# The last 64 of 320 features contracted in row pairs, in two layers of an mLSTM and mixture-of-experts kernel

## The chip, the cores and the metric

The kernel runs on one core of one Trainium2 chip. The metric is the time of one execution on the device in microseconds (us), as the median of several runs.

## The reference, cut to what matters

An mLSTM attention (batch 4, 8 heads, 768 steps, head size 40) gives 3072 tokens of 320 features. A dense layer with a leaky ReLU follows, and then a layer of 8 experts of which each token takes one:

```python
def _moe_ref(x, w_in, w_out, alpha):           # 3072 x 320, 320 x 2048, 2048 x 320
    h = x @ w_in
    g = np.maximum(h, 0.0) + alpha * np.minimum(h, 0.0)
    return g @ w_out
def _moe2_ref(x, w_gate, w_output_gate, w1, w2):   # 8 experts, 320 x 1024 and 1024 x 320
    ...
        h = np.maximum(x[mask] @ w1[e], 0.0)
        ye = h @ w2[e]
        out[mask] = gate_w[mask, None] * eom[mask, e, None] * ye
```

## The kernel before, in words

**Precision.** A product is made of three: each operand is split into a rounded high part and the rest (low part), and high times high, low times high and high times low are added in PSUM, each as one pass of TensorE over float32 operands marked float32r. Plain float32 products, as in the attention, take two passes each.

**The 320 features.** They fill two and a half blocks of 128 rows. In the two first products (`ffn1`, L928, and `slot_1`, L402) block 2 of the tokens holds the last 64 features twice: their high part in rows 0 to 63, their low part in rows 64 to 127. The weights hold the last 64 rows twice as well (`dup`, L1362). So one product over 128 rows does high and low at once, and each first product takes 8 passes (`PASSES`, L926) instead of 9:

```python
PASSES = ((0, 0, 0), (1, 1, 0), (2, 2, 0), (3, 0, 0), (4, 1, 0), (0, 0, 1), (1, 1, 1), (2, 2, 1))
```

**First phase.** The attention runs in 24 units of 128 tokens; three units make a block of 384 tokens, 8 blocks in all. For each block 16 chunks of 128 hidden features pass through the dense layer, 128 chunks in all, by these steps: `F` (`ffn1`, 8 products of 384 columns into one of two PSUM tiles `ph`), `f` (`ffn_act`, L941: ScalarE's ReLU of the negative, then VectorE's sum), `g` (`ffn_split`, L951: the high part on ScalarE, the low part on VectorE or GpSimd) and `S` (`ffn2`, L957: 9 products of 336 columns). Up to chunk 24 (`KEEP`) the activated values stand in SBUF, after that in the tile `ph`, which is then held until `g` has read it. Attention's own steps stand between these: `as` (`att_s`, L756) multiplies queries and keys over 40 rows, alternately in rows 0 to 39 and rows 64 to 103, so that neighbouring products lie in different halves of the array's rows and go to different PSUM tiles; `ah` (`att_h`, L778) takes 120 rows and `ab` (`att_b`, L853) tiles of 32 columns. The weights of the dense layer come as 64-bit words that VectorE puts together (`words`, L647) and are split into both parts, and the experts' weights are loaded, split and stored again as high and low parts in a DRAM scratch (`el`, `es`, `et`).

The order of all these steps on every engine is one written list (`ORDER`, L96), and `OTHER` (L50) names the steps that go to the less usual engine.

**Second phase.** The tokens are gathered by expert into slots of 128. A slot j runs `slot_1` (two halves of 512 hidden columns, 8 products of 512 columns each, tokens stationary, weights moving out of a ring of three experts in SBUF), then TensorE does `slot_2` of slot j-1 (24 products of 320 columns) and `slot_t` of slot j (8 transposes, L414), and `slot_x` (L381) transposes the tokens of slot j+2. The offset of the expert in the ring is a register. `next_load` (L344) fetches the next expert into the ring by two conditional loads per slot, on SyncE's queue. 28 slots run.

Of the kernel before, what the change touches and what calls it, by code (L numbers as in the profile page):

```python
# [17 lines left out]
P = 128  # L18
# [6 lines left out]
E = 8  # L25
# [3 lines left out]
EC = 3 * F2 + 8 * DM  # L29
RC = 2 * EC  # L30
R1 = 6 * F2
# [5 lines left out]
HELD = 22  # L37
PIECES = [(c, 768, c, 3 * F2) for c in range(0, 3 * F2, 768)]
PIECES += [(3 * F2 + c, 640, R1 + c, 8 * DM) for c in range(0, 8 * DM, 640)]
NPIECE = len(PIECES)  # L40
PC = 768
# [3 lines left out]
KEEP = 24  # L45
# [6 lines left out]
        4, 5, 7, 8, 10, 11, 13, 15, 19,  # L52
    ),
    "prep_kt": (
        1, 2, 3, 7, 8, 10, 13, 14, 15, 16,
    ),
    "att_y": (
        4, 5, 8, 11, 13, 16, 17, 18, 19, 20, 21, 22, 23,
    ),
    "expert_split": (  # L60
        0, 1, 8, 9, 11, 12, 13, 14, 15, 18, 19, 20, 25, 26, 27, 30, 31, 32, 33, 34, 35, 36, 37, 38, 39,
        40, 41, 42, 43, 44, 45, 46, 47, 48, 49, 50, 51, 52, 53, 54, 55, 56, 57, 58, 59, 60, 61, 62, 63,
    ),
    "att_n": (
        3, 4, 5, 8,
    ),
    "att_r": (
        5, 7,
    ),
    "att_u": (  # L70
        0, 2, 3, 4, 6,
# [4 lines left out]
        0, 4, 6, 7, 11,  # L76
    ),
    "split_wo": (
        0, 3, 6, 8, 9, 12, 15,
# [15 lines left out]

ORDER = """  # L96
load_gates load_cst lo load_sel ga do gb lo lo do do do load_wg lq gw lv lo gm gates_st do do lv so gc gv ge gs gt
so gates_d do gw gc do do do so gw do do gc gt li lo gv pt gw so do di di load_g load_g gs di li ad gv gc lg gv
load_g li ae si ah au di gs as di load_g di gs ae si ae ae do ah am pt do di an an ab aa di di ay so ay lq as si gw
ay ay log av am lo do sg lg do load_g do ad au av ab aa gc ay ay li lo ac do ay ay ay ae ax ah an so do do gw gc lq  # L100
as di di di load_g ae gw lv am ay load_g ab aa ay li pt si ae gc ac ay ay ay lv ax gv lo lo log ay load_g load_g gs
do do so load_g gv do li gs lo so gv do ac gw set_al1 do ax F gs di do F el ae gw ae di di f si lq lq lg gc di di f
ad gc di gv gv g so gs S F do lo ae gs lv do as au do av si F f am ah pt ad es g do do g do so lo do do do F an et
f f gw gc ab aa load_cst2 li li au av lo so S gw S lg ay ay di ay F gw so load_g gc ay di g gv di di di di g gv li
gs gs gc si si do do pt sg ay di S do f g S log di di si as F F li li am so di gw ah di di gv li li gc gs f gv S di
di an ad si lq f di di ab lo lg lg pt lv F au F av li load_g g S g load_g sg load_g ac si f di di aa f g gs si F F
lv lg ah S S ad ay ax ay di di di di ah ae ay ay as si do do load_g g S ae an do gw f di ay ae di gc g F am si f li
ac ax lq lq gv gs ab aa F g f ay lo pt S ae di S ae li ay ay load_g ay as lq lo di di ay g S ac ad av am so ab aa
au f si F di lg g S lq el do av lg load_g load_g di di ax do do au ah f do do do si load_g el gw F an F an gw el f
ay F ay ay so es gc gv gc gv ay lv as so gs g g f ay S gs ae es S am f ae et et bo F F lv ac el as lq g g S ae F pt  # L110
log f f F el lq g ae am ad ab ab F g ax f f load_g load_g au es et av ah F bp aa ay el ay es et S ay an pt ay aa S
S g S ad ay g f g es lv lv f ac ax au F F S ae S f et f g ay es ay load_g el av as g g pt am F el ah ay ay sg an ab
et es es S F S F et el S f lq g el ay ac lg et ad F F f g es et f g f f el S g S S S au av aa load_g el ay ay es es
ay pt ah an ax lg g ay ay pt et lg ae es F f S et g F f log ad au av g ae et as am ae S bo F f g F f load_g ae ab
aa ay el lv el S g ay es el F f as am g load_g load_g es et es et F f load_g ac ax lv ah an el el ae ae lg lg S g S
S F f g ad au av pt ah an ay es F f g ab aa F f ay ay ad au av et ae et S g el load_g el F f es ay et F f ay ay ac
ax S g es ae S g ah an F f S S et es ay ay et g lv el el bp as am F f F f el g es et pt S S ab aa ac ax g ad au av
F f F f g S g ay lq sg es es S ay lv pt F f ay el lq g F f as am S g F f et es ah an ad au av S log S g bo F f sg
et g load_g load_g ay ay el el F f lg S ae ab aa ay ay ay et S F f S g lq lq S g ae ac ax lg el S as am lv load_g
load_g load_g es et es et ay ay F f pt F f g g ab aa ae ay ac ax F f S g es ay ay ay ay S F f F f ae as am lq S g g  # L120
load_g ah an ad au av ac ax ae el F f lv pt el ae g et ab aa ay ay S es es F f et et g load_g ay F f S g as am ay
ay lv S load_g S F f g F f ah an ab aa ay S el el es ad au av lg ay ae g ay el es F f ac ax g load_g et et ah an ah
an lv es et ae bp ay ay S S S ae as am F f g F f load_g bo g ab aa ae load_g ae F f g S lq el S ac ax F f g load_g
pt S pt F f lg load_g ae as am el es lq F f S g S el g es et F f et g ay ay el F f ae ab aa g ay ay ay ay F f
load_g lv F f S lq S ad au av g g es et es et el ad au av pt ae ac ax S F f g S el el as am F f F f log g S S g es
et lg bp es et F f F f g S g S load_g el S es et F f g F f log el el ae ay ay g S S bo es F f lg F f ah an g S es
as am sg ay ay et et g F f g lq ab aa ay S F f g el el S es load_g load_g sg F f F f S g ay ad au av g es ae ac ax
et S lv et ay ay ay pt F f es F f ah an ab aa ay ay lg el ae g S g es ay lv ad au av pt S F f F f el g ac ax ah an
et es et S load_g ay ay ae g el el F f es S g lg S ad au av F f et es F f lq et et g el el ac ax bp S g S S F f g F
f S es es g F f g et S S bo as am el es F f F f g et lv pt el el et as am ab aa ay es et ay ay load_g S S g lg el  # L130
load_g first_set ah an lq ab aa el ay ay ay F f g F f S g ad au av ae es F f F f lv es g S g ac ax S S ae ay ay ay
ay as am et et es et ac ax F f g F f S el el el bp g F f ah an ab aa g es es ay ay ay ay ay F f F f S S S g g et es
et el S et el F f g F f el S es es g F f et et ac ax g S S es et F f g ld el el F f g S F f g S bo ld es F f F f S
g g route_a S F f F f S g el g S bh bh bh et ld ld ld ad au av bh ld ld bh bh bh F f ld S ld es S ld ld g es F f g
bh bh S bh bh F f g F f S et bh ld g ld S bp F f F f ld bh g bh bh bh bh S S bh route_first bh bh bh g F f
route_first2 first_rows S g F f g ld S F f F f S ld ld g S ld ld ld pt ld ld g first_x first_x S bo bp et first_1
route_b first_1 route_c first_t first_s first_tl route_c2 first_t first_tl first_s first_2 first_2 route_d first_st
first_2 first_2
# [79 lines left out]
def mlstm_moe_kernel(  # L218
# [102 lines left out]
    def ring_mm(j, q, o_, lhsT, off, col, n, start, stop):  # L321
        if off is None:
            col += j * RC
        r = ring[:, col : col + n] if off is None else ring[:, ds(off + col, n)]
        mm = T.matmul(o_, lhsT, r, start=start, stop=stop)  # L325
        if j >= NB:
            return
        if j < 2:
            for ld in loads.values():
                tc.declare_no_dep(mm.ins, ld.ins, reason="the second expert has another slot, so its place is not loaded yet")  # L330
            return
        if j < 4:
            for ld in third:
                tc.declare_no_dep(mm.ins, ld.ins, reason="the first two experts have four slots or more")
        for jj in range(j - 3, j + 3):
            for qq in range(2):
                if (jj, qq) in loads and (jj, qq) != (j - 3, q):
                    tc.declare_no_dep(mm.ins, loads[jj, qq].ins, reason="that load is for other products")
        if (j - 3, q) in loads:
            tc.add_manual_dep(mm.ins, loads[j - 3, q].ins.name, SYNC, reason="weights of this slot")  # L340
# [40 lines left out]
    def slot_x(j):  # L381
        x = slot_rows(j)
        pt = (ps_acc if j > 1 else ps_att)(f"xt_{j}")
        for k in range(3):
            T.transpose(pt[:, k * P : (k + 1) * P], x[:, k * P : (k + 1) * P], ident)
        xh = work("xh", j, [P, 384], F32R, 3)
        xl = work("xl", j, [P, 256], F32R, 3)
        A.activation(xh, pt[:, :384], AF.Copy)
        V.tensor_tensor(xl, pt[:, :256], xh[:, :256].bitcast(F32), ALU.subtract)
        V.tensor_tensor(xh[64:128, 256:], pt[64:128, 256:384], xh[64:128, 256:].bitcast(F32), ALU.subtract)  # L390
        sl_x[j] = (x, xh, xl)
# [1040 lines left out]
```

## Time and profile before

| | |
|---|---|
| median of 3 runs | 745.13 us (744.65 to 745.71) |
| profiled execution | 743.45 us, its span 741.7 us |
| granted TensorE clock, mean | 0.991 of full speed |
| busy: TensorE products, weight loads | 97%, 91% of the span |
| busy: VectorE, ScalarE, GpSimd | 62%, 50%, 25% |

The span is the time from the first to the last instruction; the execution's time has 1.75 us around it. PE is TensorE's products, PEld its weight loads, which overlap products. The recorded duration of a product includes its passage through the array, so the rate of a row of products is read from the distance of their starts, not from that duration.

### The profile page before, as it was taken

The page shows a single profiled execution, that of the slowest core. Times are in us where ns is not written, and L with a number is a line of the kernel's source. Part 1 is how long each engine was busy: PE and PEld are TensorE (multiplying, and loading weights), DVE is VectorE, ACT ScalarE, POOL GpSimd, SP SyncE. Part 2 cuts the span into 40 slices and gives each one's busy share as a digit, 9 for nine tenths or more (in the row PEclk, how much of TensorE's full clock was granted, in tenths as well). Part 3 has the DMA queues.
Part 4 walks back from the last instruction along what each step waited for, and adds up shares of the span by engine and source line. Part 5 has one row for each costly group of instructions (what it writes and reads, how often), then busy time and mean ns, then how long its engine had stood idle before and what let it go on. Part 6 is the DMA issues. An engine that isn't in the chain of part 4 may idle for free. (4 is left out here: it accounts for less than half of the span.)

```text
span 741.7 us, 18086 instructions
## 1 busy us (share of the span) xinstructions
PE 716.8 (97%) x6347; PEld 673.2 (91%) x6347; DVE 456.9 (62%) x1115; ACT 373.0 (50%) x870; POOL 183.9 (25%) x239
## 2 busy tenths in 40 slices
PE   5889999999999999999999999999999999999996
PEld 4679989999999999899999999998999999999996
DVE  6889987768676667677787877766333222332222
ACT  4767878747646546646644554433333322333232
POOL 1543455422303232100100100022222222232223
PEclk9979999999999999999999999999999999999999
DMA  8968779898897947769887788886966726911000
GB/s 249 289 208 283 222 211 293 290 287 315 260 339 240 311 156 267 247 237 308 264 283 283 247 283 319 288 299 234 421 241 265 289 103 267 420 55 39 32 14 23
DMA packets 81527, 179.57 MB, mean 242 GB/s; under 512 B 8620, under 2 KB 39209, under 8 KB 80156
## 3 DMA queue, kind: packets, MB, share of 16 engines
q1 hardware_dynamic: 77980, 169.66, 67.2%
q0 software_dynamic: 3456, 8.71, 3.5%
q8 instruction: 56, 0.92, 0.5%
q14 instruction: 35, 0.29, 0.1%
HBM read 246.29 MB, written 55.59 MB: 407 GB/s over the span
## 5 line engine op out<-in xcount | busy, mean ns | idle before, releaser
L932 PE MATMUL ph<-ring 128*128 128x384 f32 x1024 | 199.2, 343 | 3.2 <-DVE ring L954 2.7
L932 PEld LDWEIGHTS ph<-ring 128*128 128x128 f32 x1024 | 177.5, 189 | 8.4 <-DVE ring L954 5.1
L966 PE MATMUL acc<-ring 128*128 128x336 f32 x384 | 123.2, 326 | 0.2 <-ACT ring L953 0.2
L967 PE MATMUL acc<-ring 128*128 128x336 f32 x384 | 119.5, 317 | 0.0
L945 ACT ACTIVATE v<-ph 128x384 f32<-128x384 f32 x128 | 62.4, 489 | 89.4 <-PE ph L932 88.3
L445 DVE TENSOR_SCALAR yo<-po,xg 128x320 f32<-128x320 f32 x26 | 14.3, 551 | 137.4 <-PE po L325 137.4
L325 PE MATMUL po<-ring,hh 128*128 (+1 forms) x432 | 95.6, 308 | 0.0
L947 DVE SCALAR_TENSOR_TENSOR ph<-v,al,ph 128x384 f32<-128x384 f32 x104 | 63.8, 617 | 44.3 <-ACT v L945 44.0
L325 PE MATMUL p<-ring,xh 128*128 (+1 forms) x324 | 89.8, 398 | 0.0
L969 PE MATMUL acc<-ring 128*128 128x336 f32 x384 | 80.2, 317 | 0.3 <-DVE ring L954 0.3
L325 PEld LDWEIGHTS po<-ring,hh 128*128 128x128 f32 x432 | 73.2, 187 | 2.3 <-ACT hh L425 0.2
L966 PEld LDWEIGHTS acc<-ring 128*128 128x128 f32 x384 | 72.2, 188 | 2.1 <-ACT ring L953 0.5
L954 DVE TENSOR_TENSOR ring<-ph,ring 128x384 fp32r<-128x384 f32 x104 | 57.2, 553 | 26.0 <-ACT ring L953 24.6
L953 ACT ACTIVATE ring<-ph 128x384 fp32r<-128x384 f32 x104 | 50.5, 488 | 45.1 <-DVE ph L947 40.9
L425 ACT ACTIVATE hh<-p 128x512 fp32r<-128x512 f32 x54 | 29.4, 595 | 86.4 <-PE p L423 86.4
L967 PEld LDWEIGHTS acc<-ring 128*128 128x128 f32 x384 | 72.2, 188 | 0.0
L325 PEld LDWEIGHTS p<-ring,xh 128*128 128x128 f32 x324 | 58.8, 188 | 11.3
L446 POOL DMA_INDIRECT out_dram<-yo,tok x28 | 28.1, 1003 | 160.9 <-DVE yo L445 129.6
L412 ACT ACTIVATE hr<-p 128x512 f32<-128x512 f32 x56 | 33.4, 597 | 67.7 <-PE p L325 67.7
L325 PE MATMUL po<-ring,hl 128*128 (+1 forms) x216 | 66.6, 308 | 0.2 <-DVE hl L427 0.2
L969 PEld LDWEIGHTS acc<-ring 128*128 128x128 f32 x384 | 63.5, 189 | 0.6 <-DVE ring L954 0.6
L753 ACT ACTIVATE D<-D,EKT 128x128 f32<-128x128 f32 x192 | 60.7, 394 | 5.1 <-DMA D<-gd 5.0
(211 smaller groups left out, 1102.5 us busy)
## 6 DMA issues: line engine op xcount, KB each, us to landing
ring<-scr SPq DMA_DIRECT2D x26, 3072.0 KB
ring<-scr SPq DMA_DIRECT2D x26, 2560.0 KB
ring<-scr SPq DMA_DIRECT2D x33, 512.0 KB
D<-gd SPq DMA_DIRECT2D x48, 256.0 KB
er<-in_ew_dram SPq DMA_DIRECT2D x32, 384.0 KB
scr<-ring SPq DMA_DIRECT2D x32, 384.0 KB
scr<-er SPq DMA_DIRECT2D x32, 384.0 KB
er<-in_ew_dram SPq DMA_DIRECT2D x32, 320.0 KB
```

The source lines that it names most:

```text
L325: mm = T.matmul(o_, lhsT, r, start=start, stop=stop)
L412: A.activation(hr_half(j, hf), ph, AF.Relu)
L425: A.activation(hh[:, hs], pts[j, hf], AF.Copy)
L753: A.activation(d[:, j], d[:, j], AF.Exp, bias=EKT[:, c, i + j : i + j + 1])
L932: T.matmul(ph[:, :384], wi_[i][lo][:, wc], xTs[n % 2][:, xc], start=(a == 0), stop=(a == len(PASSES) - 1),)
L945: A.activation(v, ph[:, :384], AF.Relu, scale=-1.0)
L947: V.scalar_tensor_tensor(g, v, al1[:, i : i + 1], ph[:, :384], ALU.mult, ALU.add)
L953: A.activation(gh, v, AF.Copy)
L954: engine(V, G, "ffn_split", k).tensor_tensor(gl, v, gh.bitcast(F32), ALU.subtract)
L966: T.matmul(ac, gh[:, sl], hi, start=(i == 0), stop=False)
L967: T.matmul(ac, gh[:, sl], lo, start=False, stop=False)
L969: T.matmul(accs[n][t][:, :NO], gl[:, t * P : (t + 1) * P], hi, start=False, stop=(i == NFC - 1))
```

## The change

The last 64 features are no longer doubled. Weights of two halves of the output now share a block of 128 rows: rows 0 to 63 hold the last 64 features' weights for one, rows 64 to 127 for the other. The tokens' block 2 holds the last 64 features twice in the high part and twice in the low part. Three products per output (`ENDS`) run over 64 rows, those of the two outputs alternately, so that neighbours lie in different halves of the array's rows and in different PSUM tiles; six products per output (`PAIRS`) run over 128 rows. In the dense layer the two outputs are an even chunk and the odd one after it, in an expert slot the two halves of 512 columns. In slots from 2 on ScalarE first copies the ends' weights (128 x 1024) from the ring to a tile at a fixed place (`slot_e`).

With it come: smaller weights (2048 + 512 in place of 3072 columns of each part of an expert's first matrix; odd chunks of the dense layer 256 in place of 384 columns); all activated values in SBUF (`KEEP` 128); one subtraction in place of two in `att_x` and `slot_x`; more buffers for `v` and `raw`; a new `ORDER`, and new lists in `OTHER` (60 of the 128 low parts of `ffn_split` on GpSimd, 9 before). In the new order the TensorE step directly ahead of an odd chunk's `F` is `as` 9 times, `ab` 2 times and an even `F` 33 times of 64, and no even `F` follows directly on an odd one.

```diff
-EC = 3 * F2 + 8 * DM
+W1 = 2 * F2
+WE = F2 // 2
+EC = W1 + WE + 8 * DM
-HELD = 22
-PIECES = [(c, 768, c, 3 * F2) for c in range(0, 3 * F2, 768)]
+HELD = 20
+PIECES = [(0, 704, 0, W1), (704, 704, 704, W1), (1408, 640, 1408, W1), (W1, WE, 2 * W1, WE)]
-KEEP = 24
+KEEP = 128
...
+PAIRS = ((0, 0, 0), (0, 1, 0), (1, 0, 0), (1, 1, 0), (0, 0, 1), (0, 1, 1))
+ENDS = ((0, 0), (1, 0), (0, 1))
...
+    def slot_e(j):
+        at = nc.values_load(roff[0:1, j - 1 : j], engines=[ET.Activation], min_val=0, max_val=2 * RC, **KW)
+        ends[j] = we[j % 2]
+        cp_ = A.activation(ends[j], ring_at(j, at, 2 * W1, 2 * WE).bitcast(F32), AF.Copy)
+        ring_dep(j, 0, cp_.ins)
...
-        chunks = (xh[:, 0:P], xh[:, P : 2 * P], xh[:, 2 * P :], xl[:, 0:P], xl[:, P:])
+        chunks = [t[:, c * P : (c + 1) * P] for t in (xh, xl) for c in range(3)]
         for hf in halves:
             ph = ps_att(f"p1_{j}_{hf}")
-            for a, (xc, wc, lo) in enumerate(PASSES):
-                ring_mm(j, 0, ph, chunks[xc], offs[j], lo * 3 * F2 + wc * F2 + hf * 512, 512, a == 0, a == len(PASSES) - 1)
-            A.activation(hr_half(j, hf), ph, AF.Relu)
+            p1s[j, hf] = ph
+            if hf:
+                for a, (l_, lo) in enumerate(ENDS):
+                    for h_ in range(2):
+                        rows = slice(64 * h_, 64 * h_ + 64)
+                        es = slice(lo * WE, (lo + 1) * WE)
+                        r = ring_at(j, None, 2 * W1 + lo * WE, WE, rows) if j < 2 else ends[j][rows, es]
+                        mm = T.matmul(
+                            p1s[j, h_], chunks[3 * l_ + 2][rows], r, start=(h_ == 1 and a == 0), stop=(h_ == 0 and a == 2)
+                        )
+                        if j < 2:
+                            ring_dep(j, 0, mm.ins)
+                A.activation(hr_half(j, 0), p1s.pop((j, 0)), AF.Relu)
+            for a, (l_, wc, lo) in enumerate(PAIRS):
+                ring_mm(
+                    j, 0, ph, chunks[3 * l_ + wc], offs[j], lo * W1 + wc * F2 + hf * 512, 512,
+                    hf == 0 and a == 0, hf == 1 and a == len(PAIRS) - 1,
+                )
+            if hf:
+                A.activation(hr_half(j, 1), p1s.pop((j, 1)), AF.Relu)
+                ends.pop(j, None)
+                if 2 <= j and j + 1 < NB:
+                    slot_e(j + 1)
...
         def load_wi(i):
-            load_words(f"wi{i}", wi[i], 3 * P)
+            n = (3 - i % 2) * P
+            load_words(f"wi{i}", wi[i // 2, :, i % 2 * 3 * P : i % 2 * 3 * P + n], n)
...
-            V.tensor_tensor(xT[:, 3:5, cols], pv[:, 0:2], xT[:, 0:2, cols].bitcast(F32), ALU.subtract)
-            V.tensor_tensor(xT[64:128, 2, cols], pv[64:128, 2], xT[64:128, 2, cols].bitcast(F32), ALU.subtract)
+            V.tensor_tensor(xT[:, 3:6, cols], pv, xT[:, 0:3, cols].bitcast(F32), ALU.subtract)
...
         def ffn1(k):
             n, i = divmod(k, NFC)
-            ph = ps_h(f"ph_{k}")
-            for a, (xc, wc, lo) in enumerate(PASSES):
+            x = xTs[n % 2]
+            gt[k] = ps_h(f"ph_{k}")
+            odd = i % 2
+            if odd:
+                for a, (l_, lo) in enumerate(ENDS):
+                    for o in range(2):
+                        rows = slice(64 * o, 64 * o + 64)
+                        T.matmul(
+                            gt[k - 1 + o][:, :384],
+                            wi_[i - 1][lo][rows, 2],
+                            x[rows, 3 * l_ + 2],
+                            start=(o == 1 and a == 0),
+                            stop=(o == 0 and a == 2),
+                        )
+            for a, (l_, wc, lo) in enumerate(PAIRS):
                 T.matmul(
-                    ph[:, :384],
+                    gt[k][:, :384],
                     wi_[i][lo][:, wc],
-                    xTs[n % 2][:, xc],
-                    start=(a == 0),
-                    stop=(a == len(PASSES) - 1),
+                    x[:, 3 * l_ + wc],
+                    start=(odd == 0 and a == 0),
+                    stop=(odd == 1 and a == len(PAIRS) - 1),
                 )
```

## Rows read from the trace of the kernel before

**Rows 1.** The page: busy time, share of the span, instructions; granted clock in 40 slices

```profile
PE 716.8 (97%) x6347; PEld 673.2 (91%) x6347; DVE 456.9 (62%) x1115; ACT 373.0 (50%) x870; POOL 183.9 (25%) x239
...
PEclk9979999999999999999999999999999999999999
```

**Rows 2.** Busy time by stage: stage, its length, busy of each engine, clock, DMA

```profile
0.00:20.00 20.00, 9.57 (x129) 7.66 (x129) 13.02 (x40) 9.40 (x28) 4.10 (x10) 1.00 0.85 253
20.00:40.00 20.00, 17.58 (x219) 14.61 (x223) 18.50 (x42) 13.56 (x34) 10.68 (x14) 0.87 0.92 270
40.00:60.00 20.00, 17.57 (x272) 15.20 (x265) 18.06 (x47) 14.20 (x45) 8.62 (x12) 0.87 0.80 238
60.00:490.00 430.00, 426.42 (x4231) 410.27 (x4230) 324.65 (x785) 256.52 (x616) 96.95 (x134) 1.00 0.82 272
510.00:735.00 225.00, 224.83 (x1374) 206.78 (x1373) 67.98 (x144) 71.22 (x134) 56.95 (x57) 1.00 0.49 192
```

**Rows 3.** What TensorE's products waited for: total us, times, longest

```profile
PE pe_g L576 <- DVE gin L572: 6.9, 1, 6.9
PE ph L932 <- DVE ring L954: 2.7, 8, 0.7
```

**Rows 4.** Timeline of PE around one att_s: start, us, engine, line, count

```profile
302.64 1.57 PE L932 MATMUL ph<-ring 128*128 128x384 f32 x8
304.14 1.16 PE L763 MATMUL ps<-q 40*128 40x128 f32 x16
305.23 1.68 PE L932 MATMUL ph<-ring 128*128 128x384 f32 x8
306.75 0.32 PE L966 MATMUL acc<-ring 128*128 128x336 f32 x1
```

**Rows 5.** Timeline of PEld around the same att_s, two answers

```profile
302.49 1.40 PEld L932 LDWEIGHTS ph<-ring 128*128 128x128 f32 x8
304.14 0.97 PEld L763 LDWEIGHTS ps<-q 40*128 40x128 f32 x16 [0.25 <-issue]
...
304.25 0.86 PEld L763 LDWEIGHTS ps<-q 40*128 40x128 f32 x14
```

**Rows 6.** Timeline of PE around one att_h, 120 rows

```profile
168.03 0.83 PE L785 MATMUL pb<-state,qg 120*128 120x123 f32 x6
168.62 1.65 PE L932 MATMUL ph<-ring 128*128 128x384 f32 x8
170.11 0.31 PE L966 MATMUL acc<-ring 128*128 128x336 f32 x1
```

**Rows 7.** Timeline of PEld in expert slots: transposes, then products of 512 columns

```profile
604.58 0.94 PEld L423 LDWEIGHTS p<-cst,hr 128*128 128x128 f32 x8
...
606.85 1.34 PEld L325 LDWEIGHTS p<-ring,xh 128*128 128x128 f32 x6
```

**Rows 8.** Groups by line and shape: busy us, mean ns, idle before and its releaser

```profile
L945 ACT ACTIVATE v<-ph 128x384 f32<-128x384 f32 x128 | 62.4, 489 | 89.4 <-PE ph L932 88.3 <-DVE ring L954 0.8
L947 DVE SCALAR_TENSOR_TENSOR ph<-v,al,ph 128x384 f32<-128x384 f32 x104 | 63.8, 617 | 44.3 <-ACT v L945 44.0
L412 ACT ACTIVATE hr<-p 128x512 f32<-128x512 f32 x56 | 33.4, 597 | 67.7 <-PE p L325 67.7
L661 DVE SCALAR_TENSOR_TENSOR f_wi<-r_wi,f_wi 128x384 int32<-128x384 int32 x16 | 10.9, 684 | 0.4
L659 DVE SCALAR_TENSOR_TENSOR f_wi<-r_wi,f_wi 128x384 int32<-128x384 int32 x16 | 9.6, 602 | 0.2
L657 DVE TENSOR_SCALAR f_wi<-r_wi 128x384 int32<-128x384 int32 x16 | 6.3, 391 | 1.3 <-DMA r_wi<-in_wi_dram 1.2
L921 DVE TENSOR_TENSOR ring<-pt,ring 64x128 fp32r<-64x128 f32 x24 | 7.1, 295 | 0.3
```

**Rows 9.** Stages of the second phase: length, ScalarE busy, clock, DMA share, GB/s

```profile
540.00:545.00 5.00, 1.19 (x2) 1.00 0.74 309
550.00:600.00 50.00, 15.75 (x30) 1.00 0.68 264
```

**Rows 10.** The page's DMA issues: count and KB each

```profile
ring<-scr SPq DMA_DIRECT2D x26, 3072.0 KB
r_wi<-in_wi_dram SPq DMA_DIRECT2D x16, 384.0 KB
```

More of the change, by code (lines that the diff above doesn't have):

```diff
@@ L319, in mlstm_moe_kernel, with ring_at, ring_dep @@
     early = {}
-    def ring_mm(j, q, o_, lhsT, off, col, n, start, stop):
+    def ring_at(j, off, col, n, rows=slice(0, P)):
         if off is None:
-            col += j * RC
-        r = ring[:, col : col + n] if off is None else ring[:, ds(off + col, n)]
-        mm = T.matmul(o_, lhsT, r, start=start, stop=stop)
+            return ring[rows, col + j * RC : col + j * RC + n]
+        return ring[rows, ds(off + col, n)]
+    def ring_dep(j, q, ins):
         if j >= NB:
@@ L329, in ring_mm @@
             for ld in loads.values():
-                tc.declare_no_dep(mm.ins, ld.ins, reason="the second expert has another slot, so its place is not loaded yet")
+                tc.declare_no_dep(ins, ld.ins, reason="the second expert has another slot, so its place is not loaded yet")
             return
@@ L333, in ring_mm @@
             for ld in third:
-                tc.declare_no_dep(mm.ins, ld.ins, reason="the first two experts have four slots or more")
+                tc.declare_no_dep(ins, ld.ins, reason="the first two experts have four slots or more")
         for jj in range(j - 3, j + 3):
@@ L337, in ring_mm @@
                 if (jj, qq) in loads and (jj, qq) != (j - 3, q):
-                    tc.declare_no_dep(mm.ins, loads[jj, qq].ins, reason="that load is for other products")
+                    tc.declare_no_dep(ins, loads[jj, qq].ins, reason="that load is for other products")
         if (j - 3, q) in loads:
-            tc.add_manual_dep(mm.ins, loads[j - 3, q].ins.name, SYNC, reason="weights of this slot")
+            tc.add_manual_dep(ins, loads[j - 3, q].ins.name, SYNC, reason="weights of this slot")
+    def ring_mm(j, q, o_, lhsT, off, col, n, start, stop):
+        mm = T.matmul(o_, lhsT, ring_at(j, off, col, n), start=start, stop=stop)
+        ring_dep(j, q, mm.ins)
+    ends = {}
+    we = []
+    def slot_e(j):
[3 more added lines that the diff above has]
+        ring_dep(j, 0, cp_.ins)
     regs = {}
@@ L455, in slots @@
             if j < j1:
+                if j == 2 or j >= NB:
+                    slot_e(j)
                 slot_1(j)
@@ L463, in slots @@
                 slot_out(1)
-                for p_ in range(30, 33):
+                for p_ in range(27, 30):
                     early_load(p_)
@@ L1165, in route_d @@
         def route_d():
-            f = hp.tile([P, 384], F32, tag="v", bufs=2, name="slots")
+            f = hp.tile([P, 384], F32, tag="v", bufs=4, name="slots")
             se3 = f[0:1, : 32 * (E - 1)].rearrange("p (s e) -> p s e", e=E - 1)
@@ L1294, in mlstm_moe_kernel @@
     w2.append(ctx.enter_context(tc.tile_pool(name="w2", bufs=2, reuse_waits="tile")))
+    for i in range(2):
+        we.append(r2.tile([P, 2 * WE], F32R, name=f"we{i}"))
     for i in range(6):
@@ L1301, in mlstm_moe_kernel @@
             if j == 2:
-                for p_ in range(HELD, 30):
+                for p_ in range(HELD, 27):
                     ld = early_load(p_)
```

157 lines of the change are left out of this document (77 added, 80 removed), and 3 rows, old and new, of the table OTHER.

## The prediction

> **What bounds the kernel.** I read the page's engine line first: TensorE's products cover 97% of the span, and the clock is at its upper level, 2.4 GHz, in nearly every slice [rows 1]. Busy time by stage says where the rest lies: the first 60 us have 15.3 us without a product, the dense stage from 60 to 490 us has 3.6 us, the expert stage from 510 to 735 us has 0.2 us [rows 2]. The list of waits agrees: the largest is one wait of 6.9 us at the start, and the dense layer's products lose 2.7 us to held PSUM tiles [rows 3]. So from 60 us on the time is the sum of what TensorE's stream costs, product by product; VectorE is busy for 324.65 of 430 us there and ScalarE for less, so neither sets the end. The change has to be priced in TensorE's stream.
>
> **Prices of the stream.** Starts, not durations, count. Eight weight loads of the dense layer take 1.40 us with the last one lasting 0.19, so one pass of 384 columns costs (1.40 - 0.19)/7 = 0.173 us; the products' own row gives (1.57 - 0.34)/7 = 0.176 with 0.34 for the last [rows 4, 5]. I take 0.175. A pass of 512 columns costs (1.34 - 0.19)/5 = 0.230 us [rows 7].
>
> **Does a row pair cost one pass?** The kernel already has such pairs, in att_s. Fourteen weight loads, seven pairs, take 0.86 us with the last at 0.19: a pair costs 0.67/6 = 0.112 us [rows 5]. A whole-array pass with the same 128 columns, the transposes, costs (0.94 - 0.14)/7 = 0.114 us [rows 7]. So a pair costs what one pass costs, and two half products run at once. Price of a pair of ends: one pass, 0.175 us in the dense layer, 0.230 us in a slot. The other bound is no overlap, 0.35 and 0.46 us: att_s moves 128 columns in 0.112 us, 0.88 ns a column, while the ends want 0.175/384 = 0.46 ns, so no row shows two tiles filled at that rate. I stay near the pair's row, whose geometry is the same, and keep the bound for a rival. The Trainium skill (TensorE: Matmul & The Clock Gate, "Measured speedup vs the span model") gives 3.07 times for four row tiles of 32 rows and 512 columns, 77% of ideal; the trace shows 0.114/0.112, no loss, for two. By the page's figure three pairs would cost 0.68 us in place of 0.525 and 0.90 in place of 0.69, an estimate of 16 us more over the kernel.
>
> **What does entering and leaving the pairs cost?** This is where I expect the change to turn. Around one att_s, from the first product of 8 dense passes at 302.64 to the first product of the second layer at 306.75 are 4.11 us [rows 4]. In it are 16 dense passes, 16 x 0.175 = 2.80, and 8 pairs, 8 x 0.112 = 0.90: together 3.70. So 0.41 us are neither. The weight-load row shows a part of it: the first load of att_s comes 0.25 us late with no wait behind it ("issue") [rows 5], where otherwise loads run ahead under the product before. The control is att_h, also two-pass float32 but over 120 rows: from 168.03 to 170.11 are 2.08 us, against 8 x 0.175 = 1.40 and 6 x 0.112 = 0.67, 2.07 in all [rows 6]. Nothing is lost there. So it isn't the number format, it is the change between whole array and half rows, about 0.2 us each way; the other groups of att_s that I followed between dense steps show the same distances. I take 0.40 us for a round trip, with 0.33 and 0.45 as its bounds from the rounding of these rows.
>
> **The change part by part.**
> - *Dense layer.* 64 chunk pairs, 16 passes before. After: 12 whole passes and 3 pairs, 15 in price, less 0.175 us; one round trip, plus 0.40. Net 64 x (0.40 - 0.175) = +14.4 us.
> - *Merged trips.* In 9 of 64 cases att_s stands directly ahead of the odd chunk; both are in the half-row state, so one way out and one way in fall away: 9 x -0.40 = -3.6 us. The 2 with att_b I leave at nothing: they change state anyway.
> - *Expert slots.* 28 slots (56 activations of a half [rows 8]), 16 passes of 512 columns before, 15 after, and a round trip: 28 x (0.40 - 0.230) = +4.8 us.
> - *Start.* Odd chunks load and decode a third less: 8 x (0.391 + 0.602 + 0.684)/3 = 4.5 us of VectorE at most [rows 8], and 8 x 128 KB, 1 MB of the 384 KB loads [rows 10], 4 us at 253 GB/s [rows 2]. VectorE is busy for 49.6 of the first 60 us [rows 2], and the 6.9 us wait is on VectorE's gates. But half of the loss is there before any dense weight. Bounds -6 and +2; I take -2.
> - *Held PSUM tiles.* With all activated values in SBUF, the tile is free after VectorE's sum, and the 2.7 us [rows 3] go. Against it, an even chunk is now complete only with the odd chunk's ends, so a pair holds both tiles. I set these two against each other: 0, bounds -2.7 and the third rival.
> - *slot_e.* One ScalarE copy of 1024 columns per slot, under 2 x 0.597 = 1.19 us [rows 8]. ScalarE is busy for 15.75 of 50 us [rows 9], in six slots at 225/28 = 8.0 us each [rows 2]; 7.1 more leave 27 free. What is queued behind it are the two copies of hh, which are due only after slot_2's 24 products, by columns 24 x 0.175 x 320/384 = 3.5 us later. So 0. Its wait is new: it needs the next slot's weights a slot earlier, and the ring load of slot j now also waits for the copy of slot j+1. The loads of the first experts are through by 545 us, where the DMA share falls to 0.74 [rows 9], and the loads (3072 KB before, 2560 after for this part) are issued three slots ahead. 0; if a load were late, ScalarE would stand, then hh, then TensorE.
> - *att_x, slot_x, the GpSimd moves.* One VectorE instruction of 0.295 us less per unit [rows 8], against a wider one; VectorE has room in these stages, so 0. Low parts moved to GpSimd are slower but need not be ready at once; GpSimd is busy for 97 of 430 us [rows 2]. 0; a late one would hold its `S`, which the waits would name.
>
> Sum: +14.4 - 3.6 + 4.8 - 2 = +13.6 us on the profiled execution's 743.45 us, 757.0. The median of the runs lies 1.68 us above that execution, so **758.7 us**.
>
> **Rivals.**
> 1. *The change of state costs nothing for one-pass products (faster).* Place: the 92 groups of ends. If the 0.40 us belonged to two-pass operands alone, what is left is 64 x -0.175 + 28 x -0.230 - 2 = -19.6 us: 725.5 us. It decides below the price at which (64 + 28 - 9) trips equal 19.6 us, 0.24 us a trip. For it: every trip in the trace is with two-pass products on one side. Against it: dense one-pass products stand on the other side of it and start late too, and att_h, two-pass, loses nothing [rows 4, 6]. Chance 0.11. The span rule of the Trainium skill (TensorE: Matmul & The Clock Gate, "Measured speedup vs the span model"), which prices a group of tiles as one product and 4 ns for each further tile, knows no such cost and would give this outcome; another page of the Trainium skill, TensorEngine Tiling (Array Packing), "Key Properties", states that changing the tiling mode drains the engine, without a price. By that rule this rival falls, and the trace agrees: 0.41 us [rows 4].
> 2. *Half products don't overlap at one pass a column.* Then three more passes per pair and slot: 64 x 3 x 0.175 + 28 x 3 x 0.230 = +52.9, 811.6 us. Against it the pairs of att_s; for it the rate that no row shows. Chance 0.05.
> 3. *The pairs of chunks choke on two PSUM tiles.* The next even chunk needs the even tile back: ends, then 0.489 and 0.617 us of ScalarE and VectorE [rows 8], 1.1 us, against 6 x 0.175 = 1.05 us of the odd chunk and a step `S` of nine products that the order always puts between. If the two engines are behind with other work by one instruction, some 0.3 us a pair, +19 us: 778 us. Chance 0.07.
>
> **How the numbers follow.** The forecast has 0.77, the rivals 0.11, 0.05 and 0.07. The range: trips at 0.33 us and the start at -6 give 758.7 - 5.8 - 4 = 749; trips at 0.45 give +4, half of the third rival +9.5, 768 to 772, for which 770 stands. Left out are the first and second rivals and the far half of the third, just under 2 in 10. What a measurement of this kernel can tell from no change is about 0.2%, 1.5 us. Faster 0.11 (the first rival and trips under 0.24), same 0.02, slower 0.87.
>
> **What would show it.** In the changed profile: ends starting in twos a few ns apart, pairs 0.175 and 0.230 us apart (first step; twice that means rival 2); the first weight load of each group of ends and of the six passes behind it starting late with "issue" as its reason, 0.4 us a trip (second step; if the loads run ahead, rival 1); TensorE still at 97% with hardly any named waits from 60 us on (rival 3 would show waits of L932's successor on the activation). The dense stage should grow by some 11 us, the expert stage by some 5. The forecast is wrong if a trip costs under 0.3 us, or if the new order gains more than 6 us in the first 60 us.

## The result, and the profile after

The changed kernel takes 756.11 us (median of 4 runs, 755.59 to 756.42); the kernel before, run beside it, 745.42 (4 runs). The ratio is 1.0137, its 95% interval 1.0112 to 1.0162: slower by 10.2 us by the ratio, 10.7 by the medians. The forecast was 758.7, with 749 to 770 as its range and 0.87 for slower. The profiled execution took 756.32 us, its span is 754.5.

Three readings of the changed kernel come first. The page's busy time and clock (to be held against [rows 1]):

```profile
PE 727.5 (96%) x6531; PEld 645.6 (86%) x6531; DVE 408.3 (54%) x970; ACT 421.1 (56%) x1014; POOL 263.9 (35%) x313
...
PEclk9869999999999999999999999999999999999999
```

Busy time by stage, with the columns of [rows 2]:

```profile
0.00:20.00 20.00, 9.19 (x104) 7.08 (x104) 11.86 (x36) 8.62 (x22) 5.29 (x12) 1.00 0.78 235
20.00:40.00 20.00, 14.94 (x231) 12.31 (x225) 15.99 (x41) 13.86 (x36) 9.31 (x14) 0.80 0.99 288
40.00:60.00 20.00, 17.64 (x270) 14.84 (x270) 16.72 (x41) 13.66 (x46) 6.16 (x8) 0.77 0.82 237
60.00:490.00 430.00, 426.52 (x4297) 387.73 (x4296) 284.98 (x676) 278.64 (x732) 174.26 (x205) 1.00 0.74 246
510.00:735.00 225.00, 224.93 (x1406) 192.92 (x1407) 65.58 (x137) 95.72 (x158) 55.78 (x57) 1.00 0.48 182
```

What TensorE's products waited for, with the columns of [rows 3]:

```profile
PE pe_g L619 <- DVE gin L615: 5.8, 1, 5.8
PE pw L743 <- DVE f_wo L704: 4.9, 5, 2.1
PE pb L830 <- DVE ring L765: 1.9, 1, 1.9
PE pa L907 <- POOL y L942: 1.3, 1, 1.3
PE acc L1020 <- ACT ring L1007: 1.2, 1, 1.2
```

From 60 us on TensorE is as full as before: 426.52 of 430 us, where [rows 2] has 426.42, and 224.93 of 225. So the loss is no new wait; the stream itself has become longer. The clock is at its upper level, 2.4 GHz, but for some of the first 60 us, as before; there it dips lower (0.80 and 0.77 in the rows, 0.87 in [rows 2]). In a further profile of before it was 0.77 over those 60 us, and the dense layer began at 46.4 us all the same. Behind the start the clock has a small share: the changed kernel's dense layer begins with 4.5 us at the lower level, 1.2 GHz (granted 0.50 from 48.1 to 52.6 us), that of before with 1.9 us (46.7 to 48.6), TensorE busy throughout in both. That is some 1.3 us between the two profiles, an estimate: half of the 2.6 us. VectorE lost 40 us of work in the dense stage (324.65 to 284.98), which bought nothing there. In the waits, the held tile of [rows 3] (`ph` on VectorE's low part of the split, 2.7 us) is gone, and the second layer's weights `f_wo` are late for `pw` five times, 4.9 us, of which 3.9 lie ahead of the first dense product. Before has 0.8 us for that wait:

```profile
PE pw L698 <- DVE f_wo L661: 0.8, 1, 0.8
```

Where the stream grew is seen around one group of ends, 443 to 447 us. Timelines of the products and of the weight loads; start, us, engine, line, count:

```profile
443.37 1.23 PE L987 MATMUL ph<-ring 128*128 128x384 f32 x6
444.53 0.79 PE L979 MATMUL ph<-ring 64*128 64x384 f32 x6
445.25 1.31 PE L987 MATMUL ph<-ring 128*128 128x384 f32 x6
446.40 0.32 PE L1020 MATMUL acc<-ring 128*128 128x336 f32 x1
```

```profile
443.22 1.05 PEld L987 LDWEIGHTS ph<-ring 128*128 128x128 f32 x6
444.53 0.47 PEld L979 LDWEIGHTS ph<-ring 64*128 64x128 f32 x6 [0.25 <-issue]
445.25 1.00 PEld L987 LDWEIGHTS ph<-ring 128*128 128x128 f32 x6 [0.25 <-issue]
446.23 0.19 PEld L1020 LDWEIGHTS acc<-ring 128*128 128x128 f32 x1
```

From the first whole product at 443.37 to the next layer at 446.40 are 3.03 us. In it are 12 whole passes and three pairs, 15 x 0.175 = 2.63. The 0.40 us left is the round trip. It lies at the two "issue" gaps: the first weight load of the ends (444.53) and the first behind them (445.25) start 0.25 us late, though nothing named holds them, while the loads of `acc` run ahead of their products (446.23 against 446.40). Among the products' starts four steps are long, 0.26 to 0.28 us in place of 0.175: to the first and to the second product behind each change of rows. The six half products take 0.47 us of weight loads, 0.28 us from the first to the last start: they run in twos, three passes in price.

In an expert slot, where a pass has 512 columns, the gap is longer, 0.36 us (weight loads of one slot):

```profile
608.54 0.42 PEld L351 LDWEIGHTS p<-ring,xh 128*128 128x128 f32 x2
609.33 0.18 PEld L438 LDWEIGHTS p<-we,xh 64*128 64x128 f32 x2 [0.36 <-issue]
609.44 0.19 PEld L438 LDWEIGHTS p<-we,xl 64*128 64x128 f32 x2
609.67 0.19 PEld L438 LDWEIGHTS p<-we,xh 64*128 64x128 f32 x2
610.22 0.30 PEld L351 LDWEIGHTS p<-ring,xh 128*128 128x128 f32 x2 [0.36 <-issue]
```

The two traces by stage, each from the starts of products (us):

| stage | before | after | difference |
|---|---|---|---|
| up to the dense layer's first product | 46.7 | 48.1 | +1.4 |
| to the last product of its second layer | 451.0 | 458.1 | +7.1 |
| first slot's first product to the last slot's last | 237.9 | 242.7 | +4.8 |

### The profile page after: what moved, and what is told of

Its sections match the earlier page's. It is cut to its first block, busy times and chain, and to the rows that moved or that the text cites. A ratio compares the mean times of both kernels' runs of the same rounds, so it can differ in the third digit from the quotient of the medians.

```text
span 754.5 us, 18441 instructions
## 1 busy us (share of the span) xinstructions
PE 727.5 (96%) x6531; PEld 645.6 (86%) x6531; DVE 408.3 (54%) x970; ACT 421.1 (56%) x1014; POOL 263.9 (35%) x313
## 4 chain that ended last, share of the span: by engine, by line
PE 90%; DVE 5%; DMA 3%; issue 1%; ACT 1%; SPq 0%; POOL 0%; POOLq 0%; DVEq 0%
PE ph L987 19%; PE po L351 13%; PE p L351 10%; PE acc L1020 8%; PE acc L1023 7%; PE acc L1021 7%; PE ph L979 6%; PE ps L808 3%; PE p L438 3%; PE p L464 3%; PE pa L907 2%; PE pb L830 2%; DMA r_wo<-in_wo_dram 2%; PE pd L861 1%; PE xt L406 1%; PE pt L954 1%
## 5 line engine op out<-in xcount | busy, mean ns | idle before, releaser
L987 PE MATMUL ph<-ring 128*128 128x384 f32 x768 | 166.6, 352 | 0.1
L987 PEld LDWEIGHTS ph<-ring 128*128 128x128 f32 x768 | 130.6, 189 | 17.7 <-issue 15.5
L1001 DVE SCALAR_TENSOR_TENSOR v<-v,al,ph 128x384 f32<-128x384 f32 x128 | 77.0, 609 | 63.2 <-ACT v L999 59.5
L1008 POOL TENSOR_TENSOR ring<-v,ring 128x384 fp32r<-128x384 f32 x60 | 62.4, 1044 | 98.8 <-ACT ring L1007 75.0
L1007 ACT ACTIVATE ring<-v 128x384 fp32r<-128x384 f32 x128 | 66.3, 523 | 45.8 <-DVE v L1001 31.1
L351 PE MATMUL p<-ring,xh 128*128 (+1 forms) x216 | 72.3, 416 | 0.0
L1259 POOL TENSOR_TENSOR er<-er,eh 128x640 fp32r<-128x640 f32 (+2 forms) x33 | 52.5, 1596 | 34.6 <-ACT eh L1258 27.5
L799 POOL TENSOR_SCALAR_AFFINE_SELECT D<-D 128x512 f32<-128x512 f32 x48 | 31.2, 651 | 92.5 <-ACT D L798 81.7
```

The lines of the kernel that those rows point to most:

```text
L351: mm = T.matmul(o_, lhsT, ring_at(j, off, col, n), start=start, stop=stop)
L987: T.matmul(gt[k][:, :384], wi_[i][lo][:, wc], x[:, 3 * l_ + wc], start=(odd == 0 and a == 0), stop=(odd == 1 and a == len(PAIRS) - 1),)
L1001: V.scalar_tensor_tensor(g, v, al1[:, i : i + 1], ph[:, :384], ALU.mult, ALU.add)
L1007: A.activation(gh, v, AF.Copy)
L1008: engine(V, G, "ffn_split", k).tensor_tensor(gl, v, gh.bitcast(F32), ALU.subtract)
L1259: engine(G, V, "expert_split", x).tensor_tensor(st[:, :n].bitcast(F32R), st[:, :n], eh[:, :n].bitcast(F32), ALU.subtract)
```

## The experiments

"Changed" is the kernel after the change, "before" the one before it; each time stands beside before's median in runs on the same chip. A difference to changed (756.11 us) is one of medians that can come from two chips; before's median was 745.25 to 746.29 us on them.

### What one trip costs

**The ends in two visits.** Two of the three pairs go ahead of the odd chunk's whole products, the third behind two of them: the same products, one more round trip in each of 64 places.

```diff
-                for a, (l_, lo) in enumerate(ENDS):
-                    ...
+                end(0)
+                end(1)
             for a, (l_, wc, lo) in enumerate(PAIRS):
+                if odd and a == 2:
+                    end(2)
```

> The changed kernel with the same products, but the third pair of ends of each chunk pair is issued after two whole products of the odd chunk, so TensorE goes to half rows twice in each pair. Theory: 64 more trips x 0.40 = 25.6 us more than 756.1, about 782. Rival (a fixed price for each half product, whatever stands beside it): no change, 756.

Measured: 781.82 us (4 runs; ratio to before 1.0479, 1.0450 to 1.0508). That is 25.7 us over the changed kernel, 25.7/64 = 0.40 us a trip, and the rival falls. The weight loads of its two lines say where (groups by line; idle before them):

```profile
L993 PEld LDWEIGHTS ph<-ring 128*128 128x128 f32 x768 | 126.6, 189 | 30.2 <-issue 27.7 <-DVE v L1007 0.9 <-ACT ring L964 0.3
...
L979 PEld LDWEIGHTS ph<-ring 64*128 64x128 f32 x384 | 31.4, 184 | 27.8 <-issue 27.3
```

The same two groups of the changed kernel:

```profile
L987 PEld LDWEIGHTS ph<-ring 128*128 128x128 f32 x768 | 130.6, 189 | 17.7 <-issue 15.5 <-DVE v L1001 0.4 <-ACT ring L964 0.3
...
L979 PEld LDWEIGHTS ph<-ring 64*128 64x128 f32 x384 | 30.7, 187 | 11.8 <-issue 11.3
```

"Issue" grew by 12.2 us behind the ends and by 16.0 ahead of them, with as many products. (A late load stands here with its whole 0.25 us; about 0.2 of it reaches the products.)

**Seven of the nine shared trips taken apart.** In the written order `as` moves ahead of TensorE's step before it (an `S` in three places, as here, an even `F` in four), in 7 of the 9 places where it stood directly ahead of an odd chunk:

```diff
-... S as F ...
+... as S F ...
```

> The changed kernel with att_s moved ahead of the step before it in 7 of the 9 places where it stood directly ahead of an odd chunk's ends, so that a whole-array step lies between them. Theory (two groups in half rows side by side share one way in and one way out): 7 x 0.40 = +2.8 us on the changed kernel's 756.1, about 758.9. Rival (each group pays its own drain in any case): no change.

Measured: 759.36 us (5 runs; 1.0179, 1.0153 to 1.0204), 3.25 more than changed: 0.46 us for each, by the medians. Between the two profiles the dense stage grows by 2.6 us (460.8 against 458.1), 0.37 for each, and the ends' first loads are late for 13.0 us in all in place of 11.3, seven times 0.25:

```profile
L1018 PEld LDWEIGHTS ph<-ring 64*128 64x128 f32 x384 | 30.6, 187 | 13.4 <-issue 13.0
```

What it takes apart looks so in the changed kernel (weight loads): out of `att_s` at 229.67 into the ends at 230.56 there is no gap, and one trip serves both.

```profile
229.67 0.97 PEld L808 LDWEIGHTS ps<-q 40*128 40x128 f32 x16 [0.25 <-issue]
230.56 0.49 PEld L979 LDWEIGHTS ph<-ring 64*128 64x128 f32 x6
231.31 1.00 PEld L987 LDWEIGHTS ph<-ring 128*128 128x128 f32 x6 [0.26 <-issue]
```

**No trip in the dense layer.** Three whole products in place of three pairs, of the same duration:

```diff
-                    for o in range(2):
-                        rows = slice(64 * o, 64 * o + 64)
-                        T.matmul(gt[k - 1 + o][:, :384], wi_[i - 1][lo][rows, 2], x[rows, 3 * l_ + 2], ...)
+                    T.matmul(gt[k - 1][:, :384], wi_[i - 1][lo][:, 2], x[:, 3 * l_ + 2], start=False, stop=(a == 2))
```

> The changed kernel, with the three pairs of ends of each chunk pair replaced by three products over all 128 rows into the even chunk's tile (left out: the odd chunk's own ends; the even chunk gets both chunks' ends added). The number of passes in TensorE's time is the same, 15 a pair, and the order is the same; only the change to half rows and back is gone. Theory (a trip costs 0.40 us): 64 trips less the 9 shared with att_s, 55 x 0.40 = 22 us less than the changed kernel's 756.1, about 734. Rival (the lost time comes from the new order, the two held tiles or the wider ScalarE work, not from the trip): no more than 3 us away from 756.

Measured: 743.61 us (10 runs; 0.9970, 0.9951 to 0.9988), 12.5 us less than changed, not 22. Its dense stage took 444.5 us in place of 458.1. So neither the theory's sum nor the rival's 756 came out. The row from 60 to 485 us, before this kernel's dense layer ends, and three of the longest waits in it:

```profile
60.00:485.00 425.00, 416.90 (x4172) 400.98 (x4171) 286.91 (x681) 278.78 (x734) 176.33 (x208) 1.00 0.77 254
```

```profile
PE acc L1018 <- ACT ring L1005: 1.8, 1, 1.8
PE pb L830 <- DVE D L816: 1.7, 1, 1.7
PE pa L907 <- ACT ring L1005: 1.3, 1, 1.3
```

TensorE stands idle for 8.1 of 425 us, against 3.5 of 430 with the pairs. About 5 us have come back as waits, on ScalarE and VectorE, which the trips had covered. The price itself came off nearly whole. Over the last 56 chunk pairs, with 48 trips that aren't shared, the ends and the products at their edges cost 17.6 us less from start to start. This trace also has a dip of the clock there (granted 0.50 from 405 to 408 us), in which nine of these products took 2.67 us in place of 9 x 0.175 = 1.58; without it the difference is 18.7 us, 0.39 a trip.

**No trip in the slots.** The same edit in the expert slots.

```diff
-                    for h_ in range(2):
-                        ...
+                    mm = T.matmul(p1s[j, 0], chunks[3 * l_ + 2], r, start=False, stop=(a == 2))
```

> The same in the expert slots alone: three products over 128 rows into the first half's tile in place of three pairs (left out: the second half's own ends). Theory: 28 trips x 0.40 = 11.2 us less than 756.1, about 745, and a slot of 8.58 us goes to some 8.18. Rival (the slots' loss is the copy of the ends' weights or a late load): the slot stays at 8.58 us and the time at 756.

Measured: 745.18 us (10 runs; 0.9996, 0.9982 to 1.0010), 10.9 less than changed: 0.39 us a slot. Here the whole sum arrives, and the rival falls: from the first slot's first product to the last slot's last are 231.6 us in place of 242.7, and TensorE is idle for 0.5 us of them.

### How two half products run

**Three of one half, then three of the other.** The two loops over the ends change places, so that no neighbours lie in different halves, but for one.

```diff
-                for a, (l_, lo) in enumerate(ENDS):
-                    for o in range(2):
+                for o in range(2):
+                    for a, (l_, lo) in enumerate(ENDS):
```

> The changed kernel with the six ends of a chunk pair in another order: first the three of rows 0 to 63, then the three of rows 64 to 127, in place of alternately. One trip as before. Theory (neighbours in different halves run at once, neighbours in the same half one after the other): only the third and fourth product overlap, five pass times in place of three, 64 x 2 x 0.175 = 22.4 us more, about 778.5. Rival (the half products never overlapped, or all of them overlap whatever their order): no change, 756.

Measured: 756.55 us (4 runs; 1.0143, 1.0115 to 1.0171), no change. The theory fails; what holds is one half of the rival, that all overlap whatever their order. The weight loads of one group:

```profile
309.32 1.00 PEld L987 LDWEIGHTS ph<-ring 128*128 128x128 f32 x6
310.56 0.48 PEld L979 LDWEIGHTS ph<-ring 64*128 64x128 f32 x6 [0.25 <-issue]
311.29 0.82 PEld L987 LDWEIGHTS ph<-ring 128*128 128x128 f32 x5 [0.25 <-issue]
```

Six half loads take 0.48 us, as before (0.47). The products start at 310.564 and 310.575, at 310.846 and 310.856, at 311.021 and 311.031. The one that signals the even tile, third of six in the program, starts at 311.021 and is the fifth to start. (The trace names no place in the program; the signal tells which one it is.) Nor was the old order simply restored: a pair's two starts are 10 to 11 ns apart here, 3 to 4 in the changed kernel's group (444.529 and 444.532). So each half of the rows works through its own products, and the neighbours in the program need not alternate.

### What the first phase gave back

**The slots' part alone.** Before's dense layer and order, the new layout of the experts' weights, `slot_e` and the pairs in the slots.

```diff
-EC = 3 * F2 + 8 * DM
-HELD = 22
+EC = W1 + WE + 8 * DM
+HELD = 20
...
-        gsp = [(carve(384), carve(384)) for _ in range(3)]
+        gsp = [(carve(384), carve(384))]
+        gsp += [tuple(wp.tile([P, 384], F32R, name=f"gs_{i_}_{y_}") for y_ in range(2)) for i_ in range(2)]
...
+    def slot_e(j):
```

> The expert slots of the changed kernel (ends by halves, copy of the ends' weights, smaller ring and pieces) with the dense layer, the order, the split between engines and the held tiles of the kernel before. Theory: 28 x (0.40 - 0.23) = +4.8 us on the kernel before, about 750, with the slots at 8.58 us and the dense stage as before. Rival (the smaller ring and loads give something back in the first phase): nearer to 746 than to 750.

Measured: 746.37 us (12 runs) against 746.29 (20 runs): 1.0000, 0.9984 to 1.0016. In its profile the expert stage costs 243.1 us, 5.2 more than before, as it should. But the whole is no slower, so the first phase gave back about 5 us by the medians; its profile, against that of before, shows 1.1 of it. Where the rest lies is not shown.

**Values in SBUF alone**, on before, with the third buffer for `v`:

```diff
-KEEP = 24
+KEEP = 128
...
-            v = hp.tile([P, 384], F32, tag="v", bufs=2, name=f"v_{k}")
+            v = hp.tile([P, 384], F32, tag="v", bufs=3, name=f"v_{k}")
```

> The kernel before with one part of the change alone: all activated values in SBUF (KEEP 128 and three buffers v in place of two), so that a PSUM tile is free before the low part is made. Theory (this is what took the 2.7 us of waits away): up to 2.7 us less than the kernel before, 743 to 745. Rival: no change, since the order was made for the held tiles and the next step is then late instead.

Measured: 742.52 us (9 runs, 739.71 to 744.49) against 746.29: 0.9945, 0.9925 to 0.9965. By the ratio this part of the change is a gain of 4.1 us by itself (2.6 to 5.6 by the interval, which holds the 2.7 of the theory), and this kernel is faster than both. Its profile shows little of it: that execution took 744.00 us, and its dense stage 450.3 us in place of 451.0. In its waits the held `ph` of [rows 3] is gone; the largest left in the dense stage is

```profile
PE acc L966 <- ACT ring L953: 1.9, 2, 1.2
```

**Both together**: the slots' part and the values in SBUF. Of the change it leaves out the dense layer's pairs with their smaller weights, the new order with its lists in `OTHER`, and the fourth buffers of `v` and `raw` (the changed kernel has four of each, not the three of `v` that the expectation names). Its edit is the two above.

> The slots-alone kernel (746.4 us) with all activated values in SBUF and three buffers for v, as the changed kernel has them. Theory: the gain of the values in SBUF on the kernel before (3.8 us) comes on top: 742.6 us, so that pairs in the dense layer with their new order cost 13.5 us in the changed kernel (756.1), of which 64 x 0.225 = 14.4 less 9 x 0.40 = 3.6 are the trips. Rival: what was given back in the first phase of the slots-alone kernel and what the values in SBUF give are the same slack: 746 us, and the dense part costs 10.

Measured: 744.08 us (12 runs) against 745.25 (23 runs): 0.9980, 0.9967 to 0.9993. Between the two theories: on top of the slots' part the values in SBUF are worth 1.5 us by the ratios, where they gain 4.1 alone. With slots that cost 5, the first phase is about 6 us shorter than before by the medians; the profiles show 4.0 of it. And what this kernel leaves out, the dense part of the change, is the rest: 756.11 - 744.08 = 12.0 us (by the ratios, 0.0157 x 745.4 = 11.7).

**Smaller pieces of the experts' weights**, on before, to find those 5 us. The pieces to load and split are a sixth smaller; the last 64 rows are doubled by stores of 64 rows, eight of them in place of two.

```diff
-PIECES = [(c, 768, c, 3 * F2) for c in range(0, 3 * F2, 768)]
+PIECES = [(0, 704, 0, 3 * F2), (704, 704, 704, 3 * F2), (1408, 640, 1408, 3 * F2), (W1, WE, W1, 3 * F2)]
...
+            if p_ == 3:
+                for w, o in ((eh[:, :n].bitcast(F32), base), (el[:, :n], base + half)):
+                    for q in range(2):
+                        for d_ in range(2):
+                            nc.sync.dma_start(...)
```

> The kernel before with one side effect of the change alone: the experts' first matrices are loaded and split without the doubled rows (704, 704, 640 and 512 columns in place of four times 768), and only the stores to the scratch write the last rows twice. Products, ring and order are those of before. Theory (the slots alone came out level because this work, a sixth less of it on ScalarE, VectorE and GpSimd in the first phase, gives back what the slots lose): 4 to 5 us less than the kernel before, about 741.5. Rival (the first phase is set by TensorE, so smaller pieces give nothing, and the slots' +4.8 was covered by something else, such as how runs of the kernel before scatter): no change, within 1.5 us.

> The kernel before with both parts of the change that leave TensorE's stream alone: activated values in SBUF and the smaller pieces. If the two gains add up: 742.5 - 4.5, about 738. If the smaller pieces give nothing: 742 to 743, as with the values in SBUF alone.

Measured: 750.54 us (11 runs) against 745.68 (28 runs), 1.0062, 1.0040 to 1.0084; and, with the values in SBUF as well, 747.56 (12 runs), 1.0023, 1.0009 to 1.0037. Both are about 5 us worse than without the pieces. The waits of the first of the two:

```profile
PE ph L934 <- DVE ring L956: 5.8, 9, 2.1
PE pb L787 <- DMA qg<-in_qg_dram: 1.4, 1, 1.4
```

A load of attention's came late, and the held tiles cost 5.8 in place of 2.7. Two runs ask whether that is the pieces or the stores: before once more, and the same pieces with two stores over all 128 rows.

> The kernel before, unchanged, under a label of its own, for the scatter of its runs and a second profile of it. Theory: ratio 1.000, and a profile in which the expert stage has the same length to 0.1 us while the first phase differs by one to three us. Rival: both phases the same to 0.3 us, so that the difference of 2.8 us between the first profile's execution and the median of the runs has another place.

Measured: 745.80 us (12 runs), 1.0006, 0.9990 to 1.0022. The second profile (743.70 us) is like the first, more as the rival has it: the expert stage takes 237.9 us in both, and the dense layer ends at 497.8 and 497.7. Both executions lie some 2 us under their median, so where an ordinary run spends these 2 us is not shown.

The smaller pieces with two stores over all 128 rows:

```diff
+                for w, o in ((eh[:, :n].bitcast(F32), base), (el[:, :n], base + half)):
+                    nc.sync.dma_start(
+                        scr[e, :, o : o + 2 * WE].rearrange("p (d c) -> p d c", d=2),
+                        w.unsqueeze(1).to_broadcast([P, 2, WE]),
+                    )
```

> Leaves out: the last 64 rows of an expert's first matrix reach the scratch in the wrong half-row order, so the slots' last products use wrong numbers; all counts, sizes and bytes are those of the kernel before, but the loads and splits are a sixth smaller. The run with the same smaller pieces and eight stores of 64 rows took 750.5 us. Theory: the eight narrow stores per expert were what cost there, and the smaller pieces themselves are what gave back 4 to 5 us in the first phase of the slots-alone kernel: 741.5 us. Rival one: the pieces give nothing and the stores cost: 745.7, as before. Rival two: the way the pieces are cut costs whatever the stores: 750.

Measured: 744.98 us (12 runs) against 745.25: 0.9997, 0.9973 to 1.0020. So the first rival: the eight narrow stores cost about 5 us, the smaller pieces give nothing. What gave back 5 us in the slots' part stays open: left are the loads of 2560 KB in place of 3072, the stores to the scratch, a sixth smaller there and as large as before here, and the split buffers that moved to another pool. They were not tried apart. Nor was the dense part alone.

## Why the prediction was right, point by point

- **What bounds the kernel: right.** TensorE's stream, busy for 426.42 of 430 us before and for 426.52 after. The 40 us that VectorE lost in that stage bought no time.
- **A pair costs one pass: right.** Three pairs take 0.28 us between first and last load, which no serial order of six could do. The second rival (811.6 us) falls. The figure of the Trainium skill that the prediction weighed (TensorE: Matmul & The Clock Gate, "Measured speedup vs the span model"), 3.07 times for four tiles, would by the prediction's estimate have made it 16 us more; two tiles of 64 rows show no such loss here, 0.178 us from a pair to the next.
- **A trip costs 0.40 us, for one-pass products too: right**, and the step that decided the sign. 0.40 from the timeline, 0.40 from doubling the trips, 0.39 from taking them out of the slots, 0.39 from the products' starts without them in the dense layer. The first rival, faster because trips were free, falls. That changing the tiling mode drains TensorE (the Trainium skill, TensorEngine Tiling (Array Packing), "Key Properties") fits the two late loads at each group, 0.25 us each.
- **Merged trips, 9 x -0.40: right.** Seven taken apart cost 3.25 us by the medians and 2.6 by the profiles, where 2.8 were priced.
- **Expert slots, +4.8: right**, +4.8 in the profile, with the copy of `slot_e` hidden. The slot of 8.0 us is misread, since 225 us is a window and not the 28 slots: they take 237.9 us, 8.5 each. Nothing hangs on it.
- **Dense layer, +14.4 - 3.6 = +10.8: right.** From start to start the first layer's products cost 198.3 us in place of 187.7, +10.6, of which up to 1.3 are the clock's. The whole stage grew by 7.1 us, not by the "some 11" of the signs: the waits of `ph`, 2.7 us and 0.5 on VectorE's sum before, are gone from it (see the held tiles below). The changed kernel less the one without this part is 12.0 us, of which 1.3 lie ahead of the first dense product in their profiles. But the saving of 64 x 0.175 = 11.2 us shows nowhere as time: without its trips this layer leaves the kernel at 743.61 us, 0.5 under the one without the dense part (744.08). So in this order free trips would have gained little.
- **Start, -2: wrong sign, +1.4.** The step that failed is the credit for smaller odd chunks. VectorE has less to do (44.57 of 60 us against 49.58, the sums of the first three stage rows), and the wait on the gates fell from 6.9 to 5.8; but in the new order `pw` waits 4.9 us for the second layer's weights, where it waited 0.8. Work that VectorE was spared did not stand on the path; that this wait is the reason is read from the list and was not tried. The sign is no chance of one profile: the first dense product starts at 47.9 to 49.5 us in the six profiles with the new order, at 45.8 to 48.0 in the eight with the old, 48.4 against 46.8 in the mean.
- **Held PSUM tiles, 0: wrong, a gain.** I set the wait of 2.7 us off against a pair that holds two tiles. That second loss did not show: there is no wait of `ph` in the list after, so the third rival (778 us) falls, and the stage is shorter by the waits that are gone. Alone, the values in SBUF gain 4.1 us (2.6 to 5.6); whether that is more than the wait of 2.7 us they remove is not settled.
- **slot_e and the smaller weights, 0: not settled.** With the slots' part the first phase gives back about 5 us by the medians, overlapping by more than half with what the values in SBUF gain, and no run shows which part of the change does it.
- **The sum.** By the medians: 10.8 + 4.8 for the pairs, about +1.4 at the start, about -6 in the first phase, together some +11 on 745.4, 756.4 against 756.1 measured. The forecast's 758.7 lacked the -6 and had the start 3.4 too low. Profile against profile, +13.6 was forecast and +12.9 measured (756.32 - 743.45), with the slots as priced, the dense stage 3.7 too high and the start 3.4 too low: that these two cancel is luck. The forecast's 1.68 us from the execution to the median did not carry over either: the changed kernel's execution (756.32) lies at its median (756.11). Before's runs beside the experiments lie between 742.3 and 749.6, so a single profile can be 2 us off; the ratios above are safer than differences of two profiles.

So the saving was real, 15 passes for 16, but each group of ends saves one pass of 0.175 or 0.230 us and pays 0.40 for going into the half-row state and back. By these prices only the nine groups that shared a trip were ahead.

## What to carry to other kernels

A change of tile geometry has a price per visit, here 0.40 us or about two passes of 384 columns, so collect the work of that geometry into few visits, beside other steps that already use it, before counting the passes it saves. Read the price from the weight loads: a first load that starts late with nothing named ahead of it, at both ends of the group. And when a change bundles parts, run the cheap ones alone: here a buffer setting was worth some 4 us by itself, hidden behind 15 us of loss.

## What the runs showed of the hardware that was not expected

- The two halves of the rows are two streams. Three products of one half ahead of three of the other ran in twos, within 0.011 us of each other (310.564 and 310.575), the program's third starting after its fourth, and the time was the same (756.55 against 756.11).
- Eight stores of 64 rows cost about 5 us more than two of 128 rows with the same bytes (ratios to before of 1.0062 and 0.9997, medians 750.54 and 744.98). Of that 1.4 us stand in the list as a wait for a transfer, and the waits for held tiles grew from 2.7 to 5.8; how they come about was not followed.
- Trips can cover other engines. Without them in the dense layer TensorE is idle for 8.1 of 425 us in place of 3.5 of 430, and the time falls by 12.5 us where the trips cost 22.
